# A long FFT filter ahead of a maxout layer: batches 0 and 1 from 64-row to 32-row blocks

## The chip, the cores and the metric

One core of a Trainium2 chip runs the whole problem. The metric is the device time of one execution in microseconds (us). The engines of the core are TensorE (PE in the profile; its weight loads are listed apart as PEld), VectorE (DVE; `V` in the code), ScalarE (ACT; `S`), GpSimd (POOL; `G`) and SyncE (SP; `nc.sync`, which only issues DMAs here). PE writes its results to PSUM, which the kernel uses as eight banks of 128 partitions x 512 fp32.

## The reference

```python
batch, seq, dim = (8, 3072, 256)          # filt_r, filt_i: [1537, 256]
n_tokens, d_model, d_ff = (24576, 256, 1024)

X = np.fft.rfft(x, axis=1)
F = (filt_r + 1j * filt_i)[None, :, :]
y = np.fft.irfft(X * F, n=x.shape[1], axis=1)

t = y.reshape(24576, 256)
g = np.maximum(t @ w1, t @ w2)
out = g @ w_out
```

Inputs and output are fp32.

## The kernel before

**The transform.** The 3072 points of a sequence are split as 96 x 32: point 32 p + m, with p over partitions and m from 0 to 31. S1 is the 96-point transform over p, for each m (table C1; from batch 2 on a folded form with table CT). Its result has 48 columns (real and imaginary part of 48 frequencies of the 96-point transform), which the code numbers as 24 `u` of two `s` each, or as 12 `w` (or `n` pairs) x two `g` x two `s`. S2 multiplies by the twiddle factors and transforms over m, in one matmul with table U, per column: 64 input rows (real and imaginary part of 32 values) to 64 output rows (of 32 frequencies). Its result `px` lies in PSUM, one bank for each `s`. The filter is multiplied in from tile F (`pq`, `pf`, `ri`). S3 is the inverse of S2 with tables VP and VQ, S4 the inverse of S1 with G1 or G2, which leaves `y_`, 384 tokens at a time.

**The filter tile.** F is [128, 2 (real, imaginary), 12 columns w, 2 s, 256]. `load_f` brings 32 frequencies of each column to rows 64g to 64g + 31, with g of 0 or 1. `double_f` copies the same columns to rows 64g + 32 to 64g + 63 (line 164 on V for the first eight columns, four copies; four DMAs on SP for the other four).

**Two forms of S2, product and S3.** Batches 0 and 1 use the 64-row form: `s2` (line 435: eight matmuls of 64 x 64 tiles), `product` (line 441: 128 x 1024 elements, on V or, from a copy `xs` in SBUF, on POOL), and `s3` (line 459, batch 1) or `s3t` (line 772, batch 0). An output row of `px` is a real part in one 32-row half and an imaginary part in the other, and both halves meet the same filter values: so F is doubled. Batches 2 to 7 use the pair form: `s2_pairs` (64 x 32 tiles, sixteen matmuls) puts the 32 frequencies of four columns (two `w` of a pair times two `g`) into the four 32-row blocks, and real and imaginary part side by side; the filter then has to lie with the odd column of each pair in rows 64g + 32 to 64g + 63 of the even one. Between the two, in steps 47 to 59 of batch 0, `to_pairs` (five calls) moves F from one form to the other (line 479 on V, four copies 32 x 3072), copies the row of the last frequency (fN, line 472), sets one row of VQ, fills UN (the negative of a part of U) and clears one row of F.

**S3 for batch 0.** `s3t(v)` works transposed, so that its result needs no trip through DRAM: weights are 128 columns of `pq`, what moves is a table of 64 columns. Two banks `pt` are filled by 32 matmuls of 64-row tiles (line 772) and emptied at once, by ACT (line 782) or, for the last two calls' second bank, V (line 780), to `zT`. Ahead of it stand one or two matmuls of a constant (line 766, 128 x 512, here "spins") that keep PE at work. `t2` transposes zT to `zr` for `s4`.

**S3 for batch 1.** `s3(b, v)` fills two banks `pz` with 16 matmuls, ACT empties them (V the last one), and one DMA each stores to `zd` in DRAM, from where `z_read3` brings them to `zr` by SP.

**The maxout layer.** max(h1, h2) = relu(h1 - h2) + h2. So the kernel forms Wd = w1 - w2 (`prep_wd`, line 334 on POOL), M = w2 @ w_out (from the casts `cast_w2`, line 327 on POOL to w2b; `prep_t`, `prep_m`), and computes out = relu(y Wd) Wo + y M. `moe_h` (line 656) makes one of eight j of one of 64 tiles tt: two matmuls of 384 columns to `ph`, and a relu on ACT (line 661) or V (line 658) to `gt`. `moe_o` (lines 718 and 720) makes the 128-row output blocks of the tile before it, 30 matmuls for each tile. A step is one `moe_h` and its share of `moe_o`; a batch has 64 steps.

**The order.** The order on every engine is that of the program text (`manual_schedule`); nothing is moved by a scheduler. Batch 0 comes first, by itself (the opening): `s1t` and `t1` make bt[0], `table_v` and `put_v` make VP and VQ (line 315 on ACT), `double_f` completes F on V, and then come the two `s2`, `products` and `s3t` of six column groups v = 0 to 5, in an order written out by hand. `POOLED` names the v whose second product is POOL's; these, and v = 5, need `stage_x` (line 838: ACT copies px to `xs`, since POOL multiplies from SBUF). For v = 5 `shared_product` gives V 512 + 256 elements (lines 447, 448) and POOL 256 (line 449). Behind POOL's products stand in its queue `load_x(1, ...)` (line 125: x of batch 1), `load_wo`, the four `prep_wd` and the two `cast_w2`. The other batches are spread over the steps of the one before by lists of step numbers: `plan` and `later` put a call at a step, `mid` holds the visits of batch 1 (seven, in steps 25 to 46 of batch 0; each an `s3` of the group before, an `s2`, some `s1` of batch 2, and products on V), `groups` those of the later batches. PSUM: two banks in pool `pso` (po; in the opening also the tables and every second `s3t`), six in `ps`, which are taken in turn until tile 7; from there a small planner (`bk`) picks the bank that is free first.

Of the kernel before, what the change touches and what calls it, by code (L numbers as in the profile page):

```python
# [8 lines left out]
FP32 = mybir.dt.float32  # L9
# [18 lines left out]
def kernel(  # L28
# [32 lines left out]
    w2T = pfpool.tile([128, 8, D], BF16, tag="pf", name="w2T")  # L61
    UN = const.tile([128, NU // 4, 2, 32], BF16)
# [97 lines left out]
    def double_f(h, g, ri, engine):  # L160
        w0, w1 = WP[h]
        o_, i_ = F[64 * g + 32:64 * g + 64, ri, w0:w1], F[64 * g:64 * g + 32, ri, w0:w1]
        if engine is V:
            V.tensor_copy(o_, i_)  # L164
        else:
            nc.sync.dma_start(out=o_, in_=i_)
# [13 lines left out]
    def fix_f():  # L180
        V.tensor_copy(F[32:33, 0, 0, 0], FZ[32:33, 0])
# [201 lines left out]
    def s1(b, c):  # L383
# [11 lines left out]
        if b == 2:  # L395
            for g, r in ((0, 0), (1, 1), (0, 1), (1, 0)):
                TE.matmul(pa[g][64 * r:64 * r + 64], CT[64 * g:64 * g + 64, r], xb[b, c][64 * g:64 * g + 64, r],
                          start=True, stop=True)
        else:
            for r in range(2):  # L400
                for h in range(2):
                    for g in range(2):
                        TE.matmul(pa[g][64 * r + 32 * h:64 * r + 32 * h + 32], CT[64 * g:64 * g + 64, r, 32 * h:32 * h + 32],  # L403
                                  xb[b, c][64 * g:64 * g + 64, r], start=True, stop=True)
# [25 lines left out]
    def s2(b, v):  # L430
        px = [ps.tile([128, 2, D], FP32, tag="ps", name="px%d" % s) for s in range(2)]
        for i in range(2):
            for s, g in ((0, 0), (1, 1), (0, 1), (1, 0)):
                u = 2 * (2 * v + i) + g
                TE.matmul(px[s][64 * g:64 * g + 64, i], U[64 * s:64 * s + 64, u], bt[b][64 * s:64 * s + 64, u],  # L435
                          start=True, stop=True)
        return px

    def product(E, v, s, px, pool=None):
        pq = (pool or pqpool).tile([128, 2, 2, D], BF16, tag="pq", name="pq")  # L440
        E.tensor_tensor(pq, px.rearrange("p (o i) d -> p o i d", o=1).to_broadcast([128, 2, 2, D]),  # L441
                        F[:, :, 2 * v:2 * v + 2, s], OP.mult)
        return pq

    def shared_product(v, s, px, xs_, pool):
        pq = pool.tile([128, 2, 2, D], BF16, tag="pq", name="pq")
        V.tensor_tensor(pq[:, 0], px, F[:, 0, 2 * v:2 * v + 2, s], OP.mult)
        V.tensor_tensor(pq[:, 1, 0], px[:, 0], F[:, 1, 2 * v, s], OP.mult)
        G.tensor_tensor(pq[:, 1, 1], xs_[:, 1], F[:, 1, 2 * v + 1, s], OP.mult)
        return pq  # L450

    def s3(b, v, pq):
        if v == 0:
            zd[b] = dram.tile([NU, 128, D], BF16, tag="zd", name="zd")
        pz = [ps.tile([128, 2, D], FP32, tag="ps", name="pz%d" % g) for g in range(2)]
        for i in range(2):
            for q, tab in enumerate((VP, VQ)):
                for g, s in ((0, 0), (1, 1), (0, 1), (1, 0)):
                    TE.matmul(pz[g][64 * s:64 * s + 64, i], tab[64 * g:64 * g + 64, 2 * v + i, s],  # L459
                              pq[s][64 * g:64 * g + 64, q, i], start=(q == 0), stop=(q == 1))  # L460
        zt = zpool.tile([128, 2, 2, D], BF16, tag="zt", name="zt")
        for g in range(2):
            if v == 5 and g == 1:
                V.tensor_copy(zt[:, :, g], pz[g])
            else:
                S.activation(zt[:, :, g], pz[g], AF.Copy)
        nc.sync.dma_start(out=zd[b][4 * v:4 * v + 4].rearrange("u p d -> p u d"),
# [581 lines left out]
```

## Time and profile before

| | |
|---|---|
| device time, median of 3 runs | 489.45 us (489.28 to 491.54) |
| the profiled execution | 489.1 us |
| its span, first to last instruction | 487.3 us |
| mean granted TensorE clock | 0.993 |
| busy share of the span: PE, DVE, ACT, POOL | 98%, 74%, 63%, 61% |
| PE matmuls, weight loads | 6204, 6207 |
| mean DMA rate | 200 GB/s |

The profile lists one execution. A timeline row is: start in us, length in us, engine, line of the code, operation, output and input tiles with partitions x elements, and how many instructions the row joins; in square brackets stands how long the engine was idle before and what released it. A row of matmuls also has the tile of the array, as 64*32 (rows*columns). A table by stretches has the busy time of PE, PEld, DVE, ACT and POOL (with the number of instructions), then the granted clock as a share of full speed, the share of the DMA engines and GB/s. A row of the list of waits is: the waiting engine and line, what it waited for, the sum in us, how often, the longest. In a list of lines three numbers with slashes are the shortest, the median and the longest instruction in ns. One engine's busy share is an average over the opening and the steps, which have different limits.

### The profile page before, as it was taken

Reading aid. Unit: us, or ns where it says so; the run is one execution under the profiler, and the core shown is the slowest. Engines: PE = TensorE matmul, PEld = TensorE weight load, DVE = VectorE, ACT = ScalarE, POOL = GpSimd, SP = SyncE. Lnnn points to the kernel's source line nnn. Section 1 sums busy time; section 2 is a strip of 40 time slices with the busy share of each in tenths; the row PEclk is TensorE's granted clock in tenths of the full one; section 3 lists DMA queues with packets and bytes.
Section 4 is the critical chain, followed back from the end, with each engine's and each line's share of the span. In section 5 each row is a group of like instructions: output and inputs, shape, how many; then the busy total and the mean of one; then the engine's idle time right before and its main releaser. Section 6 shows DMA issues by size and latency. Waiting matters only on the chain.

```text
span 487.3 us, 15411 instructions
## 1 busy us (share of the span) xinstructions
PE 475.9 (98%) x6204; PEld 342.3 (70%) x6207; DVE 362.4 (74%) x589; ACT 307.4 (63%) x645; POOL 296.0 (61%) x378
## 2 busy tenths in 40 slices
PE   8689999999999999999999999999999999999996
PEld 4457777776677676776677676776777776777775
DVE  7886789987876878677786778777885878775542
ACT  5877488667764778468764677467774556354442
POOL 8695868559980698739874698738951266111110
PEclk9979999999999999999999999999999999999999
DMA  8999999898766889789876897789556523541112
GB/s 124 172 247 228 263 255 270 272 254 241 216 180 193 214 270 282 222 237 265 234 187 199 237 261 222 221 245 248 169 165 213 175 88 107 174 156 66 66 66 86
DMA packets 87816, 97.37 MB, mean 200 GB/s; under 512 B 9281, under 2 KB 67938, under 8 KB 87650
## 3 DMA queue, kind: packets, MB, share of 16 engines
q1 hardware_dynamic: 79010, 79.30, 57.7%
q0 software_dynamic: 8592, 17.01, 13.8%
q8 instruction: 48, 0.79, 0.7%
q14 instruction: 22, 0.18, 0.1%
q10 hardware_dynamic: 144, 0.09, 0.1%
HBM read 53.87 MB, written 47.19 MB: 207 GB/s over the span
## 4 chain that ended last, share of the span: by engine, by line
PE 93%; DVE 2%; DMA 2%; POOL 1%; issue 1%; ACT 0%; DVEq 0%; POOLq 0%
PE po L720 36%; PE ph L656 34%; PE po L718 9%; PE pc L612 3%; PE pa L403 2%; PE pz L547 2%; PE px L493 2%; DMA xb<-in_x_dram 2%; DVE pq L441 1%; DVE F L164 1%; PE pr L793 1%; POOL xb L125 1%; PE pz L459 1%; PE pa L366 1%; PE py L629 1%
## 5 line engine op out<-in xcount | busy, mean ns | idle before, releaser
L720 PE MATMUL po<-Wo,gt 128*128 128x256 bf16 x1528 | 263.1, 273 | 0.0
L661 ACT ACTIVATE gt<-ph 128x384 bf16<-128x384 f32 x347 | 165.9, 502 | 141.6 <-PE ph L656 136.8
L720 PEld LDWEIGHTS <-gt 128*128 128x128 bf16 x1528 | 144.2, 98 | 66.4 <-issue 12.4
L658 DVE TENSOR_SCALAR gt<-ph 128x384 bf16<-128x384 f32 x165 | 90.6, 552 | 46.2 <-PE ph L656 44.5
L656 PEld LDWEIGHTS <-Wd 128*128 128x128 bf16 x1024 | 99.0, 98 | 14.1 <-DVE pf L507 0.7
L668 POOL DMA_DIRECT2D out_dram<-ot x86 | 48.8, 568 | 98.1 <-DVE ot L731 87.8
L140 POOL TENSOR_TENSOR xb<-XF 128x512 bf16<-128x512 f32 x48 | 61.1, 1274 | 51.3 <-DMA XF<-in_x_dram 44.4
L503 DVE TENSOR_TENSOR pf<-px,F 128x1024 f32<-128x1024 f32 x60 | 71.1, 1218 | 18.7 <-PE px L493 7.0
L731 DVE TENSOR_SCALAR ot<-po 128x512 f32<-128x512 f32 x83 | 57.0, 686 | 18.8 <-PE po L720 18.2
L141 POOL TENSOR_TENSOR xb<-XF 128x512 bf16<-128x512 f32 x48 | 61.0, 1272 | 0.0
L407 ACT ACTIVATE at<-pa 128x512 bf16<-128x512 f32 x96 | 50.0, 603 | 4.0 <-PE pa L403 3.1
L533 POOL TENSOR_TENSOR ri<-pf 128x256 bf16<-128x256 f32 x60 | 43.8, 730 | 14.3 <-DVE pf L503 14.1
L534 POOL TENSOR_TENSOR ri<-pf 128x256 bf16<-128x256 f32 x60 | 43.6, 727 | 0.0
L556 ACT ACTIVATE zt<-pz 128x512 bf16<-128x512 f32 x60 | 31.3, 600 | 9.2 <-PE pz L547 9.2
L617 ACT ACTIVATE ce<-pc 128x384 f32<-128x384 f32 x56 | 23.7, 490 | 3.5 <-PE pc L612 2.1
L441 DVE TENSOR_TENSOR pq<-px,F 128x1024 bf16<-128x1024 f32 x19 | 22.1, 1219 | 2.6 <-PE px L435 2.3
L403 PE MATMUL pa<-xb,CT 64*32 64x512 bf16 x320 | 16.2, 381 | 0.0
L612 PEld LDWEIGHTS <-zr 48*128 48x128 bf16 x896 | 12.6, 93 | 4.4 <-issue 3.6
L612 PE MATMUL pc<-G,zr 48*128 48x48 bf16 x896 | 14.8, 180 | 0.0
L493 PE MATMUL px<-bt,U 64*32 64x256 bf16 x432 | 14.4, 272 | 0.0
L514 DVE TENSOR_TENSOR pf<-px,F 128x1024 f32<-128x1024 f32 x6 | 7.4, 1226 | 5.0 <-POOL ri L534 4.3
L804 PE MATMUL pd<-W 128*128 128x512 bf16 x26 | 9.5, 496 | 1.5 <-DVE zero L186 1.5
(415 smaller groups left out, 735.5 us busy)
## 6 DMA issues: line engine op xcount, KB each, us to landing
XF<-in_x_dram SPq DMA_DIRECT2D x96, 192.0 KB
out_dram<-ot SPq DMA_DIRECT2D x101, 128.0 KB
out_dram<-ot POOLq DMA_DIRECT2D x90, 128.0 KB, 3.5
ad<-at SPq DMA_DIRECT2D x56, 192.0 KB
zd<-zt SPq DMA_DIRECT2D x42, 256.0 KB
bt<-ad SPq DMA_DIRECT2D x72, 128.0 KB
zr<-zd SPq DMA_DIRECT2D x24, 192.0 KB
zr<-zd SPq DMA_DIRECT2D x28, 96.0 KB
```

The source lines that it names most:

```text
L140: G.tensor_tensor(t_[:, 0], f[:, 0], f[:, 1], OP.add)
L141: G.tensor_tensor(t_[:, 1], f[:, 0], f[:, 1], OP.subtract)
L407: S.activation(at[:, m0:m0 + 2], pa[g], AF.Copy)
L503: V.tensor_tensor(t_, px[s].rearrange("p (o k) d -> p o k d", o=1).to_broadcast([128, 2, 2, D]), F[:, :, 2 * n, s].rearrange("p c (o d) -> ...
L533: G.tensor_tensor(ri[:, s, 0], t_[:, 0, 0], t_[:, 1, 1], OP.subtract)
L656: TE.matmul(ph, Wd[:, dc, 128 * j:128 * j + 128], y_[:, dc], start=(dc == 0), stop=(dc == 1))
L658: V.tensor_scalar(gt[tt][:, j], ph, 0.0, None, OP.max)
L661: S.activation(gt[tt][:, j], ph, AF.Relu)
L668: E.dma_start(out=dst, in_=src)
L718: TE.matmul(p_, y_[:, n, blk], M[:, n], start=(e == 0), stop=(e == 9))
L720: TE.matmul(p_, g_[:, n - 2, blk], Wo[:, n - 2], start=(e == 0), stop=(e == 9))
L731: V.tensor_scalar(ot[tt // 2][:, e - 1:e + 1], po[q // 2 % 2], SCALE, None, OP.mult)
```

## The change

Batches 0 and 1 take the pair form as well, so that F is brought to its final form at once.

- `pair_f` takes the place of `double_f`: only the odd column of each pair is copied, 32 x 2048 elements instead of 32 x 4096 on V, and half as much in the four DMAs. `fix_f` fills fN and clears the one row of F in the opening; `to_pairs` and its five calls are gone.
- `s2_pairs` serves all batches, so U's negative UN is made in the opening: `negate_u(0, V)` among the `s1t`, `negate_u(1, S)` behind the second `sines_u`. NV, the negative of VP, is new (`negate_v`, two halves on V), and takes the third buffer of `pfpool`.
- `product` multiplies each of real and imaginary `px` by each of real and imaginary F: four products in the same 1024 elements; the one row of the last frequency gets a product by itself.
- S3 adds up the four products in PSUM, in the four PASSES (table, part of F, part of px), with tiles of 32 rows. `s3_four` does so for batch 1, four banks and 64 matmuls for two groups; `s3t` for batch 0 fills four banks over two calls, 64 matmuls each (32 before), and all four are emptied behind the second call. `z_store` of batch 1 comes one step later.
- `s1` of batch 2, too, is now in eight 64 x 32 matmuls instead of four of 64 x 64.
- The visits of batch 1 are eight instead of seven; POOLED loses group 3, and `stage_x(3)` with it; `shared_product` gives V 512 elements and POOL 512. The order of the opening is written anew.

```diff
+    NV = pfpool.tile([128, NW, 2, 64], BF16, tag="pf", name="NV")
...
-    def double_f(h, g, ri, engine):
+    def pair_f(h, g, ri, engine):
         w0, w1 = WP[h]
-        o_, i_ = F[64 * g + 32:64 * g + 64, ri, w0:w1], F[64 * g:64 * g + 32, ri, w0:w1]
+        fw = F.rearrange("p c (n r) s d -> p c n r (s d)", r=2)
+        o_ = fw[64 * g + 32:64 * g + 64, ri, w0 // 2:w1 // 2, 0]
+        i_ = fw[64 * g:64 * g + 32, ri, w0 // 2:w1 // 2, 1]
         if engine is V:
             V.tensor_copy(o_, i_)
...
     def fix_f():
-        V.tensor_copy(F[32:33, 0, 0, 0], FZ[32:33, 0])
+        V.tensor_copy(fN, FZ[32:33, 0])
+        V.memset(F[0:1, 1, 0, 0], 0.0)
...
-        if b == 2:
-            for g, r in ((0, 0), (1, 1), (0, 1), (1, 0)):
-                TE.matmul(pa[g][64 * r:64 * r + 64], CT[64 * g:64 * g + 64, r], xb[b, c][64 * g:64 * g + 64, r],
-                          start=True, stop=True)
-        else:
-            for r in range(2):
-                for h in range(2):
-                    for g in range(2):
-                        TE.matmul(pa[g][64 * r + 32 * h:64 * r + 32 * h + 32], CT[64 * g:64 * g + 64, r, 32 * h:32 * h + 32],
-                                  xb[b, c][64 * g:64 * g + 64, r], start=True, stop=True)
+        for r in range(2):
+            for h in range(2):
+                for g in range(2):
+                    TE.matmul(pa[g][64 * r + 32 * h:64 * r + 32 * h + 32], CT[64 * g:64 * g + 64, r, 32 * h:32 * h + 32],
+                              xb[b, c][64 * g:64 * g + 64, r], start=True, stop=True)
...
+    def product(E, n, s, px, pool=None):
+        pq = (pool or pqpool).tile([128, 2, 2, D], BF16, tag="pq", name="pq")
+        E.tensor_tensor(pq, px.rearrange("p (o k) d -> p o k d", o=1).to_broadcast([128, 2, 2, D]),
+                        F[:, :, 2 * n, s].rearrange("p c (o d) -> p c o d", o=1).to_broadcast([128, 2, 2, D]),
+                        OP.mult)
+        if n == 0 and s == 0:
+            E.tensor_tensor(pq[0:1, 0, 1], px[0:1, 1], fN, OP.mult)
+        return pq
+
+    def shared_product(n, s, px, xs_, pool):
+        pq = pool.tile([128, 2, 2, D], BF16, tag="pq", name="pq")
+        V.tensor_tensor(pq[:, 0], px, filt(n, s, 0), OP.mult)
+        G.tensor_tensor(pq[:, 1], xs_, filt(n, s, 1), OP.mult)
+        return pq
+
+    PASSES = ((VP, 0, 0), (NV, 1, 1), (VQ, 1, 0), (VQ, 0, 1))
+
+    def s3_four(b, k, pqs):
+        if k == 0:
+            zd[b] = dram.tile([NU, 128, D], BF16, tag="zd", name="zd")
+        pz = [ps.tile([128, 2, D], FP32, tag="ps", name="pz%d" % q) for q in range(4)]
         for i in range(2):
...
+            for a, (tab, c, m) in enumerate(PASSES):
+                for s in range(2):
+                    for q in range(4):
+                        rows = slice(32 * q, 32 * q + 32)
+                        TE.matmul(pz[q][64 * s:64 * s + 64, i], tab[rows, 4 * k + 2 * i + q % 2, s],
+                                  pqs[i][s][rows, c, m], start=(a == 0), stop=(a == 3))
         for g in range(2):
...
+            zt = zpool.tile([128, 2, 2, D], BF16, tag="zt", name="zt")
+            for r in range(2):
+                if k == 2 and g == 1:
+                    V.tensor_copy(zt[:, :, r], pz[2 * g + r])
+                else:
+                    S.activation(zt[:, :, r], pz[2 * g + r], AF.Copy)
+            later(1, z_store, b, k, g, zt)
+
+    def negate_u(h, E):
+        n0, n1 = (0, 3) if h == 0 else (3, 6)
+        i_ = U.rearrange("p (n r g) c -> p n r g c", r=2, g=2)[:, n0:n1, 1, :, 0:32]
+        if E is V:
+            V.tensor_scalar(UN[:, n0:n1], i_, -1.0, None, OP.mult)
+        else:
+            S.activation(UN[:, n0:n1], i_, AF.Copy, scale=-1.0)
+
+    def negate_v(h):
+        V.tensor_scalar(NV[:, 6 * h:6 * h + 6], VP[:, 6 * h:6 * h + 6], -1.0, None, OP.mult)
+        if h == 0:
             V.tensor_copy(VQ[0:1, 0, 0], VP[32:33, 0, 0])
...
     def s2_pairs(b, n):
-        px, kx = zip(*(bk.tile([128, 2, D], "px%d" % s) for s in range(2)))
-        bk.run(0.22)
-        for s, us in enumerate((1.14, 2.05) if n == 5 else (1.14, 1.14)):
-            bk.evict("V", us, kx[s])
+        if bk.pool is None:
+            px = [ps.tile([128, 2, D], FP32, tag="ps", name="px%d" % s) for s in range(2)]
+        else:
+            px, kx = zip(*(bk.tile([128, 2, D], "px%d" % s) for s in range(2)))
+            bk.run(0.22)
+            for s, us in enumerate((1.14, 2.05) if n == 5 else (1.14, 1.14)):
+                bk.evict("V", us, kx[s])
...
+    def visit(b, n, k, quads):
+        if k is not None:
+            s3_four(b, k, [pend.pop((b, 2 * k + i)) for i in range(2)])
+        for c in quads[0:1]:
+            s1(b + 1, c)
+        if n is not None:
+            px = s2_pairs(b, n)
             pend[b, n] = [product(V, n, s, px[s]) for s in range(2)]
+        for c in quads[1:]:
+            s1(b + 1, c)
...
+    pzt = []
+
+    def s3t(n, pq):
+        k, i = divmod(n, 2)
+        if not pzt:
+            for q in range(4):
+                pool, tag = (ps, "ps") if q > 1 else (pso, "po")
+                pzt.append(pool.tile([128, 2, 2, 2, 2, NM], FP32, tag=tag, name="pt%d" % q))
+            for _ in range(2 if k == 0 else 1):
+                TE.matmul(pzt[0].rearrange("p i s r c m -> p (i s r c m)"), W1[:, 0:128], W1, start=True, stop=True)
+            pzt.append(None)
+        else:
+            pzt.pop()
+        for s in range(2):
+            for dc in range(2):
+                for a, (tab, c, m) in enumerate(PASSES):
+                    for q in range(4):
+                        rows = slice(32 * q, 32 * q + 32)
+                        TE.matmul(pzt[q][:, i, s, :, dc], pq[s][rows, c, m, 128 * dc:128 * dc + 128],
+                                  tab[rows, 2 * n + q % 2, s].rearrange("p (r m) -> p r m", r=2),
+                                  start=(a == 0), stop=(a == 3))
+        if len(pzt) == 5:
+            return
+        zv = zT.rearrange("p c m (k i r g) q -> p k i r g (c m) q", i=2, r=2, g=2)
+        for q in range(4):
+            g, r = divmod(q, 2)
+            i_ = pzt[q].rearrange("p i s r c m -> p i (c m) (s r)")
+            if k == 2 and q % 2 == 1:
+                V.tensor_copy(zv[:, k, :, r, g], i_)
             else:
...
+                S.activation(zv[:, k, :, r, g], i_, AF.Copy)
+        del pzt[:]
...
-            double_f(1, g, ri, nc.sync)
+            pair_f(1, g, ri, nc.sync)
...
+        if c == 6:
+            negate_u(0, V)
...
-            double_f(0, g, ri, V)
+            pair_f(0, g, ri, V)
...
-    POOLED = (0, 2, 3, 4)
+    POOLED = (0, 2, 4)
...
-    pxs = {v: s2(0, v) for v in (1, 0)}
+    pxs = {v: s2_pairs(0, v) for v in (1, 0)}
     stage_x(0)
     put_v(0, 1, table_v(0, 1))
-    pxs[2] = s2(0, 2)
+    pxs[2] = s2_pairs(0, 2)
     stage_x(2)
     sines_u(1)
+    negate_u(1, S)
     put_v(1, 0, table_v(1, 0))
-    pxs[3] = s2(0, 3)
-    stage_x(3)
+    pxs[3] = s2_pairs(0, 3)
     put_v(1, 1, table_v(1, 1))
-    for v in (1, 0, 2):
+    for v in (1, 0):
         pqs[v] = products(v)
-        if v == 0:
-            load_x(1, 0, 2)
-    s3t(1, pqs[1])
-    pxs[4] = s2(0, 4)
+    negate_v(0)
+    for v in (1, 0):
+        s3t(v, pqs[v])
+    pqs[2] = products(2)
+    load_x(1, 0, 2)
+    pxs[4] = s2_pairs(0, 4)
     stage_x(4)
     pqs[3] = products(3)
-    s3t(0, pqs[0])
-    pxs[5] = s2(0, 5)
+    negate_v(1)
+    s3t(2, pqs[2])
+    pxs[5] = s2_pairs(0, 5)
     stage_x(5)
-    for v in (2, 3):
-        s3t(v, pqs[v])
-    for v in (4, 5):
-        pqs[v] = products(v)
+    pqs[4] = products(4)
+    s3t(3, pqs[3])
+    pqs[5] = products(5)
     for v in (4, 5):
         s3t(v, pqs[v])
...
-    plan_f2(0, (25, 28, 31, 35, 38, 42, 46), ((0,), (1,), (2,), (3,), (4,), (5,), (6, 7)),
+    plan_f2(0, ((25, 0, None, (0, 1)), (28, 1, None, (2,)), (32, 2, 0, ()), (35, 3, None, (3,)), (39, 4, 1, ()),
+                (42, 5, None, (4, 5)), (46, None, 2, (6,)), (48, None, None, (7,))),
             (8, 8, 10, 12, 17, 20, 24, 28), (10, 13, 16, 20, 24, 27, 30, 33))
...
-    for k, n in enumerate((47, 50, 53, 56, 59)):
-        plan(0, n, to_pairs, k)
...
```

More of the change, by code (lines that the diff above doesn't have):

```diff
@@ L439, in product @@
[L439 to L450, printed above, removed]
```

79 lines of the change are left out of this document (9 added, 70 removed).

## The prediction

> **What bounds the kernel now.** I read the page first, then busy time by stretch (busy us per engine, then granted clock, DMA share, GB/s), the list of waits between 30 and 100 us (us in total, times, longest), and the timelines of the engines up to 45 us.
>
> ```profile
> PE 475.9 (98%) x6204; PEld 342.3 (70%) x6207; DVE 362.4 (74%) x589; ACT 307.4 (63%) x645; POOL 296.0 (61%) x378
> ...
> 20.90:24.30 3.40, 1.01 (x39) 0.56 (x39) 3.18 (x4) 2.77 (x6) 1.11 (x1) 1.00 0.63 142
> 24.30:27.70 3.40, 2.72 (x89) 1.75 (x89) 3.40 (x4) 2.15 (x6) 3.39 (x3) 0.51 0.74 181
> 27.70:31.10 3.40, 3.29 (x68) 1.72 (x62) 3.40 (x4) 2.86 (x6) 3.40 (x3) 0.50 1.05 307
> 38.00:60.00 22.00, 22.00 (x206) 16.59 (x205) 14.99 (x27) 12.83 (x25) 14.65 (x17) 1.00 0.99 249
> 60.00:98.00 38.00, 38.00 (x478) 28.24 (x477) 34.34 (x46) 29.21 (x62) 25.25 (x29) 1.00 0.94 267
> ...
> PEld L656 <- POOL Wd L334: 0.5, 2, 0.2
> PEld L341 <- POOL w2b L327: 0.3, 1, 0.3
> ```
>
> From 38 us on PE is never idle: there the time is the sum of PE's work, and every us by which that stretch starts later is a us at the end. Before 38 us PE waits, at half clock from 24.3 to 31.1 us, and V and POOL are full. The two waits matter: the first main-loop matmuls already wait for POOL's Wd and w2b, so POOL's chain through the opening sets when the dense stretch gets going.
>
> The opening in the timelines (start, us, what):
>
> ```profile
> 18.27 4.74 DVE L164 COPY F<-F 32x4096 bf16<-32x4096 bf16 x4
> 23.52 8.01 DVE L441 TENSOR_TENSOR pq<-px,F 128x1024 bf16<-128x1024 f32 x7 [0.19 <-DVE F L181]
> ...
> 32.04 0.41 DVE L448 TENSOR_TENSOR pq<-px,F 128x256 bf16<-128x256 f32 x1
> ...
> 34.27 0.69 DVE L780 CAST zT<-pt 128x512 bf16<-128x512 f32 x1 [0.20 <-PE pt L772]
> ...
> 23.93 0.87 ACT L315 ACTIVATE VP<-pv 128x384 bf16<-128x384 f32 x2 [0.48 <-PE pv L301]
> ...
> 25.48 0.87 ACT L315 ACTIVATE VQ<-pv 128x384 bf16<-128x384 f32 x2 [0.18 <-PE pv L305]
> 27.41 1.09 ACT L782 ACTIVATE zT<-pt 128x512 bf16<-128x512 f32 x2 [1.07 <-PE pt L772]
> 28.39 0.60 ACT L838 ACTIVATE xs<-px 128x512 f32<-128x512 f32 x1
> ...
> 23.19 2.13 POOL L441 TENSOR_TENSOR pq<-xs,F 128x1024 bf16<-128x1024 f32 x1 [2.44 <-DVE F L164]
> 25.84 6.31 POOL L441 TENSOR_TENSOR pq<-xs,F 128x1024 bf16<-128x1024 f32 x3
> 32.11 0.66 POOL L449 TENSOR_TENSOR pq<-xs,F 128x256 bf16<-128x256 f32 x1
> 32.73 0.56 POOL L125 DMA_DIRECT2D xb<-in_x_dram  x1
> 40.16 2.02 POOL L327 CAST w2b<-WS 128x1024 bf16<-128x1024 f32 x2
> ...
> 25.38 0.61 PE L766 MATMUL pt<-W 128*128 128x512 bf16 x1
> 26.34 0.23 PE L772 MATMUL pt<-VP,pq 64*128 64x64 bf16 x2 [0.36 <-issue]
> ...
> 27.14 0.24 PE L772 MATMUL pt<-VQ,pq 64*128 64x64 bf16 x2
> 27.31 0.64 PE L435 MATMUL px<-bt,U 64*64 64x256 bf16 x8
> ```
>
> V doubles F, then multiplies without a gap; POOL waits for the doubling, then runs its products back to back up to 32.77 us, and Wd and w2b follow in its queue.
>
> **The change part by part: the opening.**
>
> ```profile
> L164 DVE COPY F<-F x4: 1209/1215/1220, 18.3 to 21.8; 32x4096 bf16<-32x4096 bf16 x4
> L479 DVE COPY F<-F x4: 950/953/956, 90.2 to 96.6; 32x3072 bf16<-32x3072 bf16 x4
> ...
> 85.90 1.26 POOL L140 TENSOR_TENSOR xb<-XF 128x512 bf16<-128x512 f32 x1 [2.12 <-DMA XF<-in_x_dram]
> 86.14 1.09 DVE L472 COPY fN<-F 1x256 bf16<-1x256 bf16 x1
> ...
> 97.65 0.77 PE L612 MATMUL pc<-G,zr 48*128 48x48 bf16 x48
> 98.35 0.39 PE L718 MATMUL po<-M,y__1893 128*128 128x256 bf16 x2
> ```
>
> V, removed: the four copies have 2048 elements instead of 4096. Each 1024 costs 1.215 - 0.953 = 0.26 us (the 3072 row is already in 512-blocks), so each saves 0.52, together 2.1 us: the products start near 21.4. V, added: the one-row fN product (under the 0.41 of the L448 row, I take 0.3), the two negations of 768 elements (0.36 each by the same slope, or, by the L472 row, up to the end of a POOL operation: that 1x256 copy ended at 87.23, when POOL's L140 did at 87.16), the 1x64 copy of VQ, and product(3, s1), 1.14 (8.01/7); gone from V is the L448 row (0.4). V ends about where it did. NV must be there when s3t first reads it, at 27.0 (below); V reaches it near 25.2, just as POOL's second product ends: cost 0, and with that cover gone at most 2.1. NV of the second half comes when POOL has nothing: cost 0. The first negate_u stands in V's gap before the bt copies, the second fits the 0.48 gap before ACT's VP row at 23.93: 0.
>
> ACT and PSUM is where I see the price. s3t now fills four banks over two calls and empties all four after the second. Follow the chain. The spins of the first s3t need the pso banks that put_v(1, 1) leaves: first half free near 25.97 (the L315 row's first of two), so the spins start at 26.05 instead of the 25.38 of the row. Two spins and the tile change took 0.96 (25.38 to 26.34), so s3t(1) starts at 27.0. Its matmuls came as pairs every 0.053 us at half clock (16 pairs, 26.34 to 27.14); four row tiles of 64 columns in the same 0.053 give 16 x 0.053 = 0.85 per call, for s3t(1) and s3t(0) together 1.7: done at 28.7, evictable at 28.94. ACT then empties four banks at 0.485 each (27.41 to 28.39 for two) before stage_x(4), in queue order: xs4 runs 30.9 to 31.5 instead of 28.39 to 28.99. Only then can POOL start product(4, s1): 31.55 instead of 30.02, 5.6 us after its load_x; it has one product fewer, but idles. Then the shared product, 512 elements instead of 256: between 0.62 spacing (256) and 2.1 (1024), 1.1. POOL is done at 34.80 instead of 32.77: 2.0 late, and load_x(1, 2, 2), load_wo, Wd and w2b behind it as well.
>
> The end of the opening on PE: s3t(5) needs the shared product (34.9), ends near 35.4, and two evictions each on ACT and V instead of one end at 36.7 instead of 34.96: 1.75. That is less than POOL's 2.0, for which PE waits at L656 and L341. So the dense stretch is 2.0 us late. Below this it is 1.75; above it 2.5, if s3t's four tiles need 20% longer.
>
> [...]
>
> **The change part by part: batch 1 in the dense stretch.**
>
> ```profile
> 67.21 0.49 PE L656 MATMUL ph<-y__1340,Wd 128*128 128x384 bf16 x2
> 67.63 0.30 PE L459 MATMUL pz<-pq,VP 64*64 64x256 bf16 x4
> ...
> 68.09 0.39 PE L435 MATMUL px<-bt,U 64*64 64x256 bf16 x8
> 68.31 0.39 PE L397 MATMUL pa<-xb,CT 64*64 64x512 bf16 x4
> 68.62 0.50 PE L720 MATMUL po<-Wo,gt 128*128 128x256 bf16 x3
> ...
> 108.19 0.41 PE L403 MATMUL pa<-xb,CT 64*32 64x512 bf16 x8
> 108.41 0.38 PE L493 MATMUL px<-bt,U 64*32 64x256 bf16 x10
> ...
> 126.47 0.32 PE L547 MATMUL pz<-ri,VP 32*64 32x256 bf16 x8
> 127.04 0.39 PE L493 MATMUL px<-bt,U 64*32 64x256 bf16 x10
> ```
>
> S2 stays at 0.22 (68.09 to 68.31); S1 in eight tiles takes 0.22 and about 0.1 to leave, as four tiles take 0.31. S3 took 0.46 for each of six (67.63 to 68.09), 2.8. Two passes of 32-row tiles take 0.57 (126.47 to 127.04), four sets of 0.11 and 0.13 for the change of tile; four passes are eight sets, 1.0, three times: 3.0. That is 0.25 more. An eighth visit adds an entry (67.21 to 67.63 is 0.42 for two L656; their 384 columns, by 0.11 for 256, need 0.33) and an exit, 0.2; tile changes inside visits 0.15. Together 0.6. The four evictions in a row (1.9 on ACT) and V's two products (2.3) hold banks that the next visit, three steps on, takes: 0 to 0.5, I take 0.1, since by the bank order only the zr copy at the visit of step 35 comes within 0.1. to_pairs (5 V operations and more) goes from steps where V waits anyway: 0 gained. SP: z_store comes a step (about 0.8 us) later; 0, since zr's reader s4g is several steps off.
>
> Sum: 2.0 + 0.6 + 0.1 = 2.7. The profiled execution took 489.1 (span 487.3, 1.8 around it): 491.8. The median shown is 489.45, 0.35 higher: 492.15. I state 492.0.
>
> **The rivals.** *Weight loads in line.* The 48 matmuls of L612 took 0.70 (97.65 to 98.35), 29 ns for two row tiles whose 48 columns, by 0.11 for 256, need 20. If 128-column weights are loaded one after another, at half clock 27 ns each, four row tiles need 0.107 a set: s3t(1) and s3t(0) cost 1.7 more, the tail 0.2: 493.7. Against it: the same 29 ns can be a floor per tile. [...]
>
> *The clock does not come back.* In stretches of 3.4 us, 2.72 busy did not bring it back, 3.29 did; it fell after 1.01. With the waits for ACT near 29.3, PE has about 2.9 in 27.7 to 31.1, between the two. If it stays at half until 38 to 41 us, the last s3t, t2, s4(0) and the first L656 run at half: 2.2 more, 494.0. [...]
>
> *V stays last (not slower).* V starts its products 2.1 earlier and was full up to 32.46; POOL loses a product (2.1) and gains 0.5. If ACT's four evictions do not hold up xs4 (spins and s3t at full clock, 1.3 less, decide it), POOL ends within 0.7 of before and the last evictions too: 489.1 + 0.5 + 0.7 = 490.3. For it: V and F L164 stand in the chain of waits now. Against: ACT's queue order. Even all of POOL's 1.6 gained would give 489.1 - 1.6 + 0.7 = 488.2, no 0.5%.
>
> *Not what it says:* the copies could fail to halve; the L479 row excludes it.
>
> **How the numbers follow.** Forecast 0.48 (491.0 to 493.0), loads in line 0.16, clock 0.12, V last 0.19 (488.2 to 491.0), a gain in the dense stretch that I cannot name 0.05. What a measurement tells from no change is about 0.5%, above 491.9 or below 487.0. Of the forecast 0.65 lies above 491.9: slower 0.31 + 0.16 + 0.12 = 0.59, same 0.36, faster 0.05. Range 489.4 to 494.8: it leaves out the lower quarter of V last (0.05), the unnamed gain, and 0.1 above.
>
> **What would show it.** Right: V's first product near 21.4; xs4 near 31; POOL idle from about 25.7 to 31.5 and done near 34.8; first L656 near 39.2; PE dense from there, three pz blocks of 1.0 us. Wrong: xs4 before 30 (chain), s3t over 1.2 us at half clock (loads in line), half clock after 31.2, gaps of PE at the visits of steps 32 to 48, or a first L656 at or before 37.8.

## The result and the profile after

The changed kernel took 505.13 us (median of 6 runs, 499.43 to 506.98) against 489.6 of the kernel before (6 runs, 489.28 to 491.71): a ratio of 1.0277, 95% interval 1.0218 to 1.0337; this ratio is of the means of the fast runs, and leaves the slowest of the six out. It is slower, as forecast, but by six times as much. The profiled execution is that slowest one, 506.98 us with a span of 505.2, so 17.9 more than that of before; the shortest run lost 10.

The page of the changed kernel, busy time of each engine and the DMA queue that carries instructions; then the same queue on the page of before:

```profile
PE 482.2 (95%) x6618; PEld 344.8 (68%) x6620; DVE 358.2 (71%) x590; ACT 306.3 (61%) x643; POOL 293.7 (58%) x377
...
q8 instruction: 52, 0.85, 0.7%
```

```profile
q8 instruction: 48, 0.79, 0.7%
```

PE's busy time grew by 6.3 us (482.2 to 475.9), in part because its clock is at half for longer (below); the other 11.6 is PE standing still. PE has 827 more instructions (matmuls and weight loads), and four more packets come in by the queue q8.

Where in time: the starts of the sixteen L657 matmuls of one tile of the changed kernel, first and last start (the tiles 0, 3, 7, 13), and those of the kernel before (L656):

```profile
L657 PE MATMUL ph<-y__1245,Wd x16: 323/326/524, 48.7 to 53.5; 128*128 128x384 bf16 x16
...
L657 PE MATMUL ph<-y__1582,Wd x16: 323/326/327, 72.2 to 79.8; 128*128 128x384 bf16 x16
...
L657 PE MATMUL ph<-y__2456,Wd x16: 326/326/326, 107.5 to 113.9; 128*128 128x384 bf16 x16
...
L657 PE MATMUL ph<-y__2762,Wd x16: 326/326/326, 153.6 to 160.1; 128*128 128x384 bf16 x16
```

```profile
L656 PE MATMUL ph<-y__1003,Wd x16: 322/326/332, 37.2 to 41.0; 128*128 128x384 bf16 x16
...
L656 PE MATMUL ph<-y__1340,Wd x16: 323/326/328, 59.9 to 67.4; 128*128 128x384 bf16 x16
...
L656 PE MATMUL ph<-y__2042,Wd x16: 326/326/326, 93.4 to 99.6; 128*128 128x384 bf16 x16
...
L656 PE MATMUL ph<-y__2351,Wd x16: 326/326/326, 136.3 to 142.7; 128*128 128x384 bf16 x16
```

The main loop starts 11.5 us late (48.7 to 37.2). Tiles 0 to 2 take 0.8 more (granted clock 0.51 until 51 us), tiles 3 to 6, with the visits of batch 1, 1.8 (35.3 to 33.5), tiles 7 to 12 3.2 (46.1 to 42.9), all the rest 0.6.

The opening by stretches, then the waits from 30 to 100 us:

```profile
31.10:36.60 5.50, 0.42 (x40) 0.30 (x33) 1.82 (x2) 0.68 (x2) 5.34 (x5) 0.75 0.87 273
36.60:39.80 3.20, 2.51 (x128) 1.87 (x128) 0.00 (x0) 2.07 (x4) 3.20 (x5) 0.50 1.13 185
39.80:43.30 3.50, 0.08 (x8) 0.00 (x0) 0.00 (x0) 0.00 (x0) 3.50 (x4) 0.50 1.25 212
43.30:48.70 5.40, 4.40 (x54) 2.80 (x55) 2.96 (x5) 2.83 (x6) 1.23 (x4) 0.50 0.32 66
```

```profile
DVE zT L791 <- PE pt L781: 11.0, 1, 11.0
...
PE pt L781 <- issue: 8.6, 2, 5.1
```

PE stops twice, for 5.1 and 3.5 us, with V and ACT idle beside it: they wait for PE. PE itself waits for "issue": no engine and no semaphore that the profile shows holds it back. PE's timeline around the two stops:

```profile
31.33 0.19 PE L781 MATMUL pt<-VP,pq 32*128 32x64 bf16 x1
36.64 0.23 PE L781 MATMUL pt<-VP,pq 32*128 32x64 bf16 x3 [5.12 <-issue]
...
37.90 0.58 PE L772 MATMUL pt<-W 128*128 128x512 bf16 x1 [0.65 <-ACT zT L793]
...
39.58 0.30 PE L781 MATMUL pt<-VQ,pq 32*128 32x64 bf16 x8
43.39 0.24 PE L781 MATMUL pt<-VP,pq 32*128 32x64 bf16 x4 [3.50 <-issue]
```

The first stop falls inside a group of four like matmuls (one before it, three behind). And the L781 matmuls alone, by stretches (their time and count, then their weight loads, granted clock, DMA share and GB/s); the first row ends before the first stop is over, the other two lie between the stops:

```profile
31.08:36.50 5.42, 0.43 (x33) 0.31 (x33) 0.76 0.86 274
...
36.60:37.80 1.20, 0.61 (x31) 0.45 (x31) 0.50 0.91 181
37.80:39.90 2.10, 1.47 (x96) 1.31 (x96) 0.50 1.27 187
```

Between the stops PE ran 31 + 96 of them and the one spin of L772: 128 matmuls and 128 weight loads, 256 instructions. A packet of q8 has 16,384 bytes, 64 for each of 256 instructions, and 13,238 instructions make 51.7 such blocks, for 52 packets (before: 48.5, for 48). So PE stops where one block of its program ends and the next has not come. The DMA queues between 28.8 and 34.2 us, and between 34.2 and 35.4:

```profile
q1 hardware_dynamic: 957, 1.87, 99.2%
```

```profile
q1 hardware_dynamic: 96, 0.17, 37.0%
q8 instruction: 1, 0.02, 5.2%
```

The first stretch moves 1.87 MB of w1 and w2, and no instruction. The block comes as they drain: the record of its packet lasts from 34.30 to 35.31, and 0.17 MB of them move behind 34.2. From the end of the first stop to the second block's packet (41.15 to 42.09) other transfers move, which the POOL queue issues (x of batch 1 and Wo); DMA queues between 36.6 and 41.1 us:

```profile
q0 software_dynamic: 1073, 0.83, 121.1%
```

A fetch did not always wait for the last load in the queues, though. In the kernel before, 0.90 MB of w1 and w2 (q1) moved only after the fetch of the table's first row had landed (31.43 to 36 us):

```profile
q1 hardware_dynamic: 473, 0.90, 54.2%
```

How the queues share the DMA engines is not shown. From the records of the packets and of PE, for blocks that PE's program has in the opening (us; an instruction's number counts PE's from the start, and the blocks begin 256 apart). No record shows when a fetch is asked for. I take the entry of the block before, as theory "instructions" does in the expectations, and that is an estimate; in the steps up to 290 us the packet's record begins within 3 us of it, in this table from 0.8 us before (second row) to 5.5 us after it (third row):

| | block before entered | fetch lands | last matmul of the block before | next matmul |
|---|---|---|---|---|
| before, instruction 963 | 27.31 | 31.43 | 32.85 | 32.88 |
| after, instruction 963 | 26.71 | 27.37 | 28.53 | 28.80 |
| after, instruction 1219 | 28.80 | 35.31 | 31.33 | 36.64 |
| after, instruction 1475 | 36.64 | 42.09 | 39.65 | 43.39 |

PE went on 1.3 us after a late block had landed (35.31 to 36.64, 42.09 to 43.39). Before, a block lasted 5.5 us at this place (27.31 to 32.85) and the fetch 4.1, with these 1.3 behind it: by this estimate it was enough by 0.1. In the changed s3t a block lasts 2.5 us (28.80 to 31.33), and the fetch takes 6.5 + 1.3.

### The profile page after: what moved, and what is told of

Same layout as the page of the kernel before. It is cut to its first block, busy times and chain, and to the rows that moved or that the text cites. A ratio compares the mean times of both kernels' runs of the same rounds, so it can differ in the third digit from the quotient of the medians.

```text
span 505.2 us, 16240 instructions
## 1 busy us (share of the span) xinstructions
PE 482.2 (95%) x6618; PEld 344.8 (68%) x6620; DVE 358.2 (71%) x590; ACT 306.3 (61%) x643; POOL 293.7 (58%) x377
## 4 chain that ended last, share of the span: by engine, by line
PE 69%; DVE 0%; ACT 0%; issue 0%
PE po L721 28%; PE ph L657 26%; PE po L719 7%; PE pc L613 2%; PE pa L402 2%; PE pz L548 2%; PE px L494 2%; PE pl L691 0%; ACT gt L662 0%; DVE gt L659 0%; DVE ot L697 0%; PE pl L689 0%
## 5 line engine op out<-in xcount | busy, mean ns | idle before, releaser
L657 PEld LDWEIGHTS <-Wd 128*128 128x128 bf16 x1024 | 99.5, 98 | 14.4 <-DVE pf L508 0.9
L504 DVE TENSOR_TENSOR pf<-px,F 128x1024 f32<-128x1024 f32 x60 | 71.4, 1219 | 22.1 <-PE px L494 6.3
L732 DVE TENSOR_SCALAR ot<-po 128x512 f32<-128x512 f32 x83 | 57.0, 686 | 19.0 <-PE po L721 17.9
L557 ACT ACTIVATE zt<-pz 128x512 bf16<-128x512 f32 x60 | 31.3, 601 | 10.8 <-PE pz L548 10.8
L431 DVE TENSOR_TENSOR pq<-px,F 128x1024 bf16<-128x1024 f32 x20 | 23.6, 1217 | 3.7 <-PE px L494 3.6
L494 PE MATMUL px<-bt,U 64*32 64x256 bf16 x576 | 20.9, 278 | 1.5 <-ACT VQ L319 0.7
L402 PE MATMUL pa<-xb,CT 64*32 64x512 bf16 x384 | 20.5, 382 | 0.4 <-POOL xb L142 0.4
L494 PEld LDWEIGHTS <-U 64*32 64x32 bf16 x576 | 9.0, 90 | 8.8 <-issue 6.1
L494 PE MATMUL px<-bt,UN 64*32 64x256 bf16 x192 | 14.0, 275 | 0.0
```

Of the source, the lines that this page charges most:

```text
L494: TE.matmul(px[s][32 * q:32 * q + 32, k], tab, bt[b][rows, u], start=True, stop=True)
L504: V.tensor_tensor(t_, px[s].rearrange("p (o k) d -> p o k d", o=1).to_broadcast([128, 2, 2, D]), F[:, :, 2 * n, s].rearrange("p c (o d) -> ...
L657: TE.matmul(ph, Wd[:, dc, 128 * j:128 * j + 128], y_[:, dc], start=(dc == 0), stop=(dc == 1))
L732: V.tensor_scalar(ot[tt // 2][:, e - 1:e + 1], po[q // 2 % 2], SCALE, None, OP.mult)
```

## The experiments

The theory "instructions" is the one above. Its rival "tiles" says that s3t with four 32-row tiles stalls by itself. Every ratio is to the kernel before, which was measured beside the run.

**Other numbers for the same instructions.** The changed kernel, and the one before, with one-column matmuls among the first ones (`tiny(n)`: n matmuls of 32 x 32 weights and one column). after_shift, then before_shift:

```diff
-    spin(12)
+    spin(10)
+    tiny(32)
...
-    spin(12)
+    spin(8)
+    tiny(96)
```

> The changed kernel with 32 one-column matmuls (64 PE instructions) among the first ones, in place of two of the twelve constant matmuls: every later PE instruction has a number higher by 64. Theory 'instructions': the holes stay at the same instruction numbers (1219 and 1475), so the first one moves 32 matmuls earlier, out of s3t(3) into the S2 of group 5 ahead of it; the products of group 5 come late as well; 5 us or more each, 502 to 512. Theory 'tiles': the hole stays at the same matmul of s3t(3), 499 to 507.

> The kernel before with 96 one-column matmuls (192 PE instructions) among the first ones, in place of four of the twelve constant matmuls: the ends of the blocks fall on other matmuls. Nothing else is changed, and there is no 32-row s3t. Theory 'instructions': the block that begins at instruction 1219 is now asked for near 29 us, inside the w1 and w2 loads, and is needed at 33.7: a hole of 1 to 4 us in s3t(4), and 490.5 to 494. Theory 'tiles': no hole, 489 to 490.

after_shift: 500.8 us (1.0223, 1.0208 to 1.0238). before_shift: 493.27 (1.0062, 1.0041 to 1.0082). PE's timelines of the two, first after_shift, then before_shift:

```profile
33.55 0.23 PE L781 MATMUL pt<-VP,pq 32*128 32x64 bf16 x3
36.73 0.23 PE L781 MATMUL pt<-VP,pq 32*128 32x64 bf16 x1 [2.95 <-issue]
```

```profile
35.56 0.19 PE L772 MATMUL pt<-VP,pq 64*128 64x64 bf16 x1
37.46 0.20 PE L772 MATMUL pt<-VP,pq 64*128 64x64 bf16 x1 [1.71 <-issue]
```

In after, 33 matmuls of s3t(3) ran ahead of the stop; here it is 3. The edit adds 32 matmuls and takes 2 spins away, so 30: the stop moved with the instruction's number, exactly (the expectation forgot the two spins, and so put it into S2). Another stop, of 1.3 us, stands 128 matmuls ahead of it, at instruction 963, and none at 1475, so which boundaries stop differs from after. In before_shift the stop of 1.7 us stands in the old 64-row s3t, between two matmuls of one pair, at instruction 1219. "Tiles" falls, by the places: the time of after_shift by itself, 500.8, lies below what "instructions" expected (502 to 512) and inside what "tiles" did; that of before_shift lies where "instructions" expected it.

**The loads of w1 and w2 at another time.** Early from V's third transpose on; late behind its last product; split, half and half. The edit of the late one (the memset makes the loads wait for V):

```diff
-    for h in range(2):
-        load_w(h)
     spin(12)
...
     pqs[5] = products(5)
+    V.memset(WS[0:1].rearrange("p (q c) (h j) -> p q c h j", q=2, h=2)[:, :, 0:1, :, 0:1], 0.0)
+    for h in range(2):
+        load_w(h)
```

> The changed kernel with one thing moved: the loads of w1 and w2 (2 MB) start from about 17 us, when V has copied the first transposes, ahead of the DMAs that complete F, instead of behind them. Theory 'instructions': PE's instructions come in blocks of 256 by a DMA that is asked for when the block before is entered; in 28 to 34 us it stands behind the w1 and w2 loads, so PE stops at the end of a block in s3t (5.3 us from 31.3, 3.7 us from 39.7). With the loads done before 28 us both holes shrink to 1 us or less, the first L657 comes at 39 to 41 us instead of 48.7, and the time is 491 to 495. Theory 'tiles': s3t with four 32-row tiles stalls by itself (banks, weight loads); the holes stay, and the time is 499 to 507.

> The kernel before with the same move of the w1 and w2 loads. Control for what the earlier loads are worth by themselves. Theory 'instructions': the fetch of the block that s3t needs at 32.9 us landed at 31.4, so there is no hole to take away: 488.5 to 490.5. Theory 'tiles': the same. Were it clearly faster, the gain of the changed kernel with this move would not be the fetch's alone.

> The changed kernel with the loads of w1 and w2 held back until V has done its last product of the opening (about 33 us), instead of starting near 26 us. Theory 'instructions': no fetch of 27 to 33 us finds them in front of it, so no hole over 0.5 us is left between 27 and 42 us; the first L657 comes at 39 to 41 us, and 493 to 496: 489.1, the 2.4 us by which the opening was late beside the holes, 1.8 of batch 1 in tiles 3 to 6, and about 1 of tiles 7 to 12. Theory 'tiles': the holes stay, 499 or more.

> Control: the kernel before with its w1 and w2 loads held back in the same way. It has no hole to lose; Wd may come up to 2 us later. Both theories: 489 to 492.

> The changed kernel with half of the w1 and w2 loads (1 MB) from about 17 us, ahead of the DMAs that complete F, and the other half held back until V's products of group 4 (about 30.5 us). Theory 'instructions': the fetch asked for near 28.8 us finds little in front of it, the one asked for near 31.3 us at most 1 MB (3 us): holes of 0.5 to 2.5 us in sum instead of 9, the first main matmul at 40 to 43 us, 493 to 498. Theory 'tiles': 499 or more.

> Control: the kernel before with its w1 and w2 loads split in the same way (second half held back until V's product of group 3). Both theories: 488.5 to 494, no gain over 0.3%.

| w1 and w2 | after: us, ratio | before: us, ratio | difference |
|---|---|---|---|
| in place | 505.13, 1.0277 (1.0218 to 1.0337) | 489.6 | 15.5 |
| early | 502.35, 1.0264 (1.0237 to 1.029) | 494.64, 1.0094 (1.0079 to 1.0109) | 7.7 |
| late | 504.67, 1.0303 (1.028 to 1.0326) | 499.26, 1.0195 (1.0171 to 1.022) | 5.4 |
| split | 503.41, 1.0256 (1.022 to 1.0292) | 492.65, 1.0062 (1.0043 to 1.0082) | 10.8 |

The times that were expected did not come. The stops did shrink; PE and then POOL of after_w_late:

```profile
32.46 0.20 PE L781 MATMUL pt<-VP,pq 32*128 32x64 bf16 x3 [0.59 <-issue]
...
35.91 0.21 PE L781 MATMUL pt<-VP,pq 32*128 32x64 bf16 x4 [0.92 <-issue]
```

```profile
43.46 1.26 POOL L338 TENSOR_TENSOR Wd<-WS 128x512 bf16<-128x512 f32 x1 [7.18 <-DMA WS<-in_moe_w_dram]
```

1.5 us of stops are left of 8.6, but now Wd waits 7.2 us for its loads, and 7.3 in before_w_late. Of the other two, early keeps stops of 3.8 us (in S2, at instruction 963) and 0.9, split of 2.3 and 2.1. Early loads are nearly all in by 28 us, but hold up the filter, whose last copies run until past 32; the fetch lands among them, at 31.8. Against its own control the change costs 5.4 us where the stops are nearly gone; both kernels wait for w1 and w2 there, which hides what else the opening would cost. No run takes the stops away and leaves all else as it was.

**Fewer instructions.** Two of the four passes of batch 0's s3t are left out, the products with the imaginary part of px:

```diff
-                for a, (tab, c, m) in enumerate(PASSES):
+                for a, (tab, c, m) in enumerate(PASSES[0::2]):
```

> The changed kernel with two of the four passes of batch 0's s3t left out (the products with the imaginary part of px, so batch 0's output is another one): 32 matmuls with four 32-row tiles a call instead of 64, as many instructions as before; the four evictions and all else stay. Theory 'instructions': the block of instruction 963 is entered near 31 us with its fetch long landed, the next one is not needed before 40 us: no hole over 0.5 us in 27 to 40 us, the first main matmul at 38 to 40 us, and 491 to 494.5 (489.1, up to 2 of the opening, 1.8 of batch 1, up to 1 of tiles 7 to 12). Theory 'tiles': s3t with four tiles still stalls, at half the count 2 us or more in each of two holes: 496 or more.

495.46 us (1.0108, 1.0079 to 1.0137), a little over what "instructions" expected, and the first main matmul at 40.2, 2.9 later than before. No stop over 0.5 us was expected, but one is left:

```profile
32.83 0.20 PE L781 MATMUL pt<-VP,pq 32*128 32x64 bf16 x3 [1.49 <-issue]
```

The block before was entered at 27.6 and the fetch landed at 31.4, as late as in the kernel before, and PE was there at 31.1. So in these two kernels the length of a stop follows from both: how long the block lasts (3.5 us here, 27.6 to 31.1, against 2.5) and how long its fetch takes (3.8 against 6.5).

**The loads in smaller pieces.** 16 DMAs of 128 KB in place of 4 of 512 KB.

> The changed kernel with the w1 and w2 loads cut into 16 DMAs of 32 partitions (128 KB) in place of 4 of 512 KB, at the same place: SP issues one in 0.45 us, so less stands queued at a time. Theory 'instructions', if the fetch waits for what has been issued: the fetch asked for at 28.8 us lands by 32 instead of 35.3, each hole under 1.5 us, 491 to 498. If the fetch has to wait for the whole load all the same (the DMA engines are full until it ends): holes of 3 to 5 us as before, 499 to 507.

500.61 us (1.0212, 1.0174 to 1.025). The fetch landed at 33.9 instead of 35.3; stops of 2.9 and 1.3 us remained: between the two expectations.

**ACT's queue, and SP's.** S2 of group 4 and stage_x(4) ahead of s3t(0) (xs4), and zr's later rows read later (z order), each on the late loads; both together also on the split and the cut loads.

```diff
-    for v in (1, 0):
-        s3t(v, pqs[v])
-    pqs[2] = products(2)
-    load_x(1, 0, 2)
+    s3t(1, pqs[1])
     pxs[4] = s2_pairs(0, 4)
     stage_x(4)
+    s3t(0, pqs[0])
+    pqs[2] = products(2)
+    load_x(1, 0, 2)
...
-        for n, u0, u1, m0, m1 in ((43, 0, 16, 0, 16), (49, 16, 24, 0, 12), (50, 0, 16, 16, 24), (51, 16, 24, 12, 24),
+        for n, u0, u1, m0, m1 in ((43, 0, 16, 0, 16), (49, 0, 16, 16, 24), (52, 16, 24, 0, 12), (53, 16, 24, 12, 24),
```

> As after_w_late, with S2 of group 4 and stage_x(4) ahead of s3t(0), so that ACT copies xs4 before the four evictions. Theory 'ACT' (the prediction's chain): POOL's product of group 4 starts near 29 us instead of 31.3, POOL ends about 2 us earlier, and the dense stretch starts up to 2 us earlier: 1 to 2 us below after_w_late. Rival: the dense stretch waits for something else (the w1 and w2 loads behind Wd): same as after_w_late within 0.4 us, though POOL's product starts early.

> As after_w_late, with the reads of zr of batch 1 in another order (the rows that the third group stores last are read three steps later), so that SP does not stand before a store that has not landed. Theory 'SP': the reads waited 6.9 us on SP, the loads of batch 3 behind them came 4 to 7 steps later than before, POOL's folds and sums with them, and the S3 of batch 2 waited in tile 12; with this order tiles 7 to 12 lose under 0.5 us and the time is 0.5 to 2 us below after_w_late. Theory 'no part of SP': as after_w_late within 0.4 us.

> As after_w_split, with S2 of group 4 and stage_x(4) ahead of s3t(0), and the reads of zr in the other order. Theory 'ACT' (the prediction's chain): POOL's product of group 4 starts 2 us earlier and, if Wd no longer waits for its loads, the dense stretch up to 2 us earlier; with tiles 7 to 12 back at the times of before 1 to 3 us below after_w_split. Rival: Wd's loads still end last, and nothing is gained in the opening: within 0.5 us of after_w_split but for tiles 7 to 12.

> As after_w_pieces, with S2 of group 4 and stage_x(4) ahead of s3t(0), and the reads of zr in the other order. If the holes are gone, the opening is up to 2 us shorter (the prediction's chain over ACT) and tiles 7 to 12 lose under 0.5: 1 to 3 us below after_w_pieces. If they are not, within 1 us of it.

after_xs4: 504.71 us against 504.67 of after_w_late. POOL, with the copy early:

```profile
29.45 2.12 POOL L431 TENSOR_TENSOR pq<-xs,F 128x1024 bf16<-128x1024 f32 x1 [3.27 <-ACT xs L850]
...
45.43 1.26 POOL L338 TENSOR_TENSOR Wd<-WS 128x512 bf16<-128x512 f32 x1 [10.32 <-DMA WS<-in_moe_w_dram]
```

The product starts at 29.45 instead of 31.6, so the order of ACT's queue was what held it; nothing is gained since Wd waits for the loads: the rival's case. after_z_order: 503.74 (502.44 to 506.19), within the scatter of after_w_late (503.18 to 505.49). Tile 12 lost 1.0 us in after_w_late and nothing here, but nothing in after_xs4 either. after_w_split_all: 500.55 against 503.41, but in the profiled executions the main loop starts at 46.4 instead of 46.9, and the gain lies in tiles 7 to 12 (43.0 instead of 47.5): the opening gains little, the rival's case again. after_pieces_all: 501.21 against 500.61; there tiles 7 to 12 lost 3.7 with the new order of the reads. So what costs time in tiles 7 to 12 (0 to 4.7 us from run to run) is not settled.

**Batch 1 alone.** The opening of before, F brought to pairs early in the steps, and the changed visits: first by copies on V (steps 14 to 23), then by DMAs (steps 9 and 10).

```diff
-            V.tensor_copy(Fw[64 * g + 32:64 * g + 64, c, :, 0], Fw[64 * g + 32:64 * g + 64, c, :, 1])
+            G.dma_start(out=Fw[64 * g + 32:64 * g + 64, c, :, 0], in_=Fw[64 * g + 32:64 * g + 64, c, :, 1])
...
-    for k, n in enumerate((47, 50, 53, 56, 59)):
+    for k, n in enumerate((9, 9, 9, 10, 10)):
```

> The kernel before, opening untouched, with the changed batch 1 alone: F is brought to pairs in steps 14 to 23, and the eight visits with s2_pairs, s3_four and the later z_store follow. Theory 'two parts': the opening's 11.5 us (9 of them holes) and batch 1 add up; here the first main matmul comes at 37.3 as before, tiles 3 to 6 take 1.8 more (S3 0.3, an eighth visit and exits 0.4, waits for banks 0.9 or more), tiles 7 to 12 at most 1: 491 to 492.5. Rival 'late SP': the later stores delay the loads of batch 3 whatever the opening does, and tiles 7 to 12 lose 1.5 to 3.5 us here too: 493 to 495. Prediction on record: 0.6 for batch 1, 490.2.

> The changed batch 1 alone again, on the opening of before. In before_b1_pairs one of V's copies of F took 5.36 us beside POOL's folds, which stopped PE for 5.6 us: here the four copies of F are DMAs from POOL's queue in steps 9 and 10, and V makes NV at step 9, when POOL computes nothing. Theory 'two parts': tiles 3 to 6 cost 1.8 (S3 0.3, an eighth visit and exits 0.4, banks 0.9 or more), tiles 7 to 12 under 0.5, since the opening is on time: 491 to 492.5. Rival 'late SP': the stores one step later delay the loads of batch 3 by themselves, and tiles 7 to 12 lose 1 to 3.5: 492.5 to 495. Prediction on record: 0.6, so 490.2.

501.86 us (1.0249, 1.0229 to 1.0268) and 496.99 (1.0133, 1.0118 to 1.0148): both above either theory, by stops that the edit itself brought. In the first V's copy took 5.36 us (below); in the second S2 of batch 1 waited 2.9 us for the DMA of its input; that the added DMAs delayed it is likely, not shown:

```profile
PE px L524 <- DMA bt<-ad: 2.9, 1, 2.9
```

What the runs do give is the price of the visits: tiles 4, 5 and 6 take 1.55, 0.85 and 0.45 us more than before in both of them, as in after and, within 0.02, in every other run of the changed batch 1 (tile 3, where these two stop, takes 1.07 less in after: with it 1.8). Tiles 7 to 12 lost 0 and 1.0.

In the openings of all these executions, before's edits as well, every stop of PE over 0.5 us with "issue" as its reason stands at instruction 963, 1219 or 1475, within two matmuls.

No version was faster than the kernel before.

## Why the prediction was wrong

**The opening up to ACT's evictions: right.** V, ACT and POOL of the changed kernel:

```profile
18.00 2.60 DVE L167 COPY F<-F 32x2048 bf16<-32x2048 bf16 x4
...
21.09 3.49 DVE L431 TENSOR_TENSOR pq<-px,F 128x1024 bf16<-128x1024 f32 x3
...
28.63 2.07 ACT L793 ACTIVATE zT<-pt 128x512 bf16<-128x512 f32 x4 [2.54 <-PE pt L781]
30.55 1.29 ACT L852 ACTIVATE xs<-px 128x512 f32<-128x512 f32 x2
...
31.26 2.13 POOL L431 TENSOR_TENSOR pq<-xs,F 128x1024 bf16<-128x1024 f32 x1 [5.75 <-ACT xs L852]
33.35 1.15 POOL L441 TENSOR_TENSOR pq<-xs,F 128x512 bf16<-128x512 f32 x1
```

The copies save 2.1, V's products start at 21.1 (forecast 21.4), the four evictions start at 28.6 (28.9), xs4 at 30.55 (30.9), POOL's product at 31.26 (31.55), and POOL is done at 34.5 (34.8). That four row tiles need no more than the 0.053 us of a pair was the author's assumption, and no row of before shows it; in its place the changed kernel shows s3t(1) and s3t(0) at 1.8 us together (26.71 to 28.53; forecast 1.7), so the rival "weight loads in line" falls, which wanted 3.4.

**"s3t(5) needs the shared product, ends near 35.4": wrong, and this is the step that failed.** The sum priced the 32 added matmuls of each call by PE's time alone, and took the arrival of PE's instructions for free. s3t(3) began at 31.1 and stopped in its middle; the evictions expected to end at 36.7 ended at 45.3. V's row, then the matmul behind the last s3t, after and before:

```profile
44.06 1.29 DVE L791 CAST zT<-pt 128x512 bf16<-128x512 f32 x2 [11.03 <-PE pt L781]
```

```profile
43.93 0.66 PE L370 MATMUL pa<-xb,C 96*96 96x512 bf16 x1
```

```profile
34.13 0.42 PE L366 MATMUL pa<-xb,C 96*96 96x512 bf16 x1
```

The two stops are 8.6 of the opening's 11.5 us. Another 1.2 arose by the end of the last s3t (43.93 instead of 34.13, 9.8 in all). The last 1.7 lies between there and the first main matmul (4.8 us instead of 3.1), at a granted clock of 0.50 where the kernel before had 1.00. So the half clock of the rival "the clock does not come back" is there too, and was priced near (2.2), but not as the rival had it: the clock had come back (0.96 from 30.7 to 34.1; in the kernel before, 0.50 from 27.7 to 31.1 and 0.99 from 31.1 to 34.5) and was at 0.50 from 34.1, inside the first stop, to 48.7. POOL's 2.0 did not decide: its last Wd was ready at 41.9, 6.8 us ahead of the first L657.

**Batch 1: 1.8 for 0.6.** PE's timeline of the changed kernel in the visit of step 42 (S1, S2, S1), and the S3 in that of step 46:

```profile
93.08 0.41 PE L402 MATMUL pa<-xb,CT 64*32 64x512 bf16 x8
93.31 0.27 PE L494 MATMUL px<-bt,U 64*32 64x256 bf16 x1
93.73 0.38 PE L494 MATMUL px<-bt,U 64*32 64x256 bf16 x9 [0.15 <-ACT gt L662]
...
94.03 0.60 PE L402 MATMUL pa<-xb,CT 64*32 64x512 bf16 x8
94.56 0.39 PE L721 MATMUL po<-Wo,gt 128*128 128x256 bf16 x2
...
97.97 0.32 PE L455 MATMUL pz<-pq,VP 32*64 32x256 bf16 x8
...
98.97 0.41 PE L402 MATMUL pa<-xb,CT 64*32 64x512 bf16 x8
```

S3 is as forecast: 1.0 (97.97 to 98.97). The bank wait, 0.1 in the sum, is the term mis-sized: S2 takes 0.72 in this visit (93.31 to 94.03) where 0.22 is its work, and the second S1 0.53 (94.03 to 94.56) instead of 0.34. Waits of this kind in the visits of steps 25, 39 and 42 make about 1.0 in the same timeline, S3 0.3, and the eighth visit with its entries and exits the rest. The sum looked for them at the copies of zr; they stand in visits that take six banks in a row (S1, S2, S1, or S3 and S2).

**SP: 0, open.** In this execution tiles 7 to 12 lost 3.2 us. In after_xs4 and after_half_s3t, with the same later stores of batch 1, they took 42.9 us as before: the stores alone are not the cause, and what is stays open.

**V did not stay last:** its last product ended at 33.0, and then it waited 11.0 us for PE. Whether POOL's queue behind ACT would have been last without the stops, no run shows.

**The range:** it begins at 489.4, which leaves out 1.2 of the 2.8 us of "V stays last" (488.2 to 491.0), over 0.4 of it and not a quarter. Nothing in the result hangs on it.

## What to carry to other kernels

PE's instructions are a stream in the DMA queues too, here of 16,384 bytes for every 256: where many small matmuls follow each other, count how long 256 of them last (2.5 us in the changed s3t) against the time until the next have come (6.5 + 1.3), and look for what the DMA queues move then. An idle engine with "issue" as the reason, in the middle of a group of like instructions, is worth a count to the next such stop. Splitting s3t's matmuls into row tiles half as high doubled its instructions (32 matmuls a call to 64), which a sum of PE's time does not show; and moving the loads that a fetch collides with out of the way is no gain where something else waits for them: in after_w_late 1.5 us of stops were left of 8.6, but Wd waited 7.2 us.

## What the runs showed of the hardware

In the openings of the table a fetch of 256 PE instructions landed 0.7 to 6.5 us after the block before was entered, and its packet's own record lasted 0.9 to 1.5. PE went on 1.3 us after a late one in the changed kernel, 1.4 in after_half_s3t (31.4 to 32.83). The kernel before stands at the edge of it, by the 0.1 above: its opening had no stop in the execution shown, but 0.9 us at instruction 963 in before_b1_pairs2, where it is unchanged:

```profile
34.30 0.20 PE L803 MATMUL pt<-VQ,pq 64*128 64x64 bf16 x2 [0.90 <-issue]
```

V's copy of F beside POOL, in before_b1_pairs, V's row and then POOL's last fold beside it:

```profile
61.40 5.36 DVE L507 COPY F<-F 32x3072 bf16<-32x3072 bf16 x1
```

```profile
64.66 1.27 POOL L142 TENSOR_TENSOR xb<-XF 128x512 bf16<-128x512 f32 x1
```

The other three copies take 0.95 us each. This one began while POOL worked through four folds without a gap, one DMA issue among them (60.42 to 65.93), and ended 0.8 us after the last of them. Another, at 58.76, took 0.95 us beside two DMA issues of POOL (59.03 to 60.40). That POOL's folds held V up is an estimate from these times. The price was PE's 5.3 us (63.7 to 69.0), for the tile that V should have scaled.
